# A late piece's stores as operations of their own, and a new order for the second half of a fast block product

## The chip, the cores and the metric

The kernel runs on one core of a Trainium2 chip. The core has a tensor engine (PE), a vector engine (DVE), a scalar engine (ACT, ScalarE), GpSimd (POOL), a queue that mostly issues transfers (SP, SyncE), and 16 DMA engines. Each engine runs its own list of instructions in order; semaphores make one wait for another. The metric is the time of one execution in device microseconds, lower being better.

## The reference

Two stages, one fed by the other. The first is attention with a polynomial sketch: for 4 batches, 4 heads, 1088 positions and 32 dimensions, queries and keys become 64 products of 8 + 8 projections, and

```python
a = np.einsum('rd,bhsd->bhsr', S1, x)
b = np.einsum('rd,bhsd->bhsr', S2, x)
phi = np.einsum('bhsi,bhsj->bhsij', a, b).reshape(*x.shape[:-1], r * r)
...
num = np.einsum('bhsf,bhfd->bhsd', q_p, kv)
den = np.einsum('bhsf,bhf->bhs', q_p, z)[..., None] + 1e-06
```

The quotient, laid out as (batch, 1088, 128), is the x of the second stage, which mixes positions with two matrices of 1088 by 1088:

```python
theta = x @ w_theta
zr, zi = x * np.cos(theta), x * np.sin(theta)
y = np.einsum('ts,bsd->btd', w_tok_r, zr) + np.einsum('ts,bsd->btd', w_tok_i, zi)
u = x + y
out = u + np.maximum(u @ w_ch, 0.0)
```

## The kernel before

The positions are cut into 8 full chunks of 128 and a tail of 64. The two mixing matrices are read as 17 rows of weights (8 of the real, 8 of the imaginary part, one row with both tails), kept in the chip's memory as `rows[i]`. Batches 0 and 1 are mixed directly: 17 products of each span of 384 positions add up in an accumulator bank (`mix_row`), a copy of the sum gets x added by a transfer that accumulates (`join`), and `finish` multiplies by `w_ch`, applies the relu and stores.

Batches 2 and 3 (`PAIR`) are mixed together by `winograd`, which replaces eight block products by seven. It splits the output positions into two halves of 544 (`HT`) and the sources into real and imaginary parts. `zsub` makes differences of the z blocks, `asum` sums and differences of the weight blocks (both on DVE), `product` runs each of the seven block products as two parts of widths 384 and 160 (`PARTS`), eight steps each, in an accumulator bank, and `add` adds a finished bank to x on DVE. Products 1 and 2, then 5, 6, 3, 7 and 4 follow from each other through the banks and the blocks that they reuse. `done(b, h)` calls `finish` for half h of batch b, in pieces of 384 and 160 positions. `finish` runs a product with `w_ch` on PE, a relu with add on DVE (L319), a turn on DVE (`turn`, L1240) and stores of 32 columns each (`store`, L1236). Batch 3's half 0 is special: its piece of 160 goes through `finish_turned` (turns on PE at L1274, a copy on ACT at L1281, relu, two plain stores at L1286), and for its piece of 384, with which the kernel ends, `ends` is true, and the stores are issued inside the same operation as the turn, one on ScalarE, one on SyncE, two on GpSimd.

In the turned batches (1 to 3) x is brought into place through memory: a DVE transpose, a store to `far` on SyncE (L1098) and a fetch of four transfers on SyncE (`fetch`, L1102). DVE multiplies it by the cosine and the sine; that is the z of `winograd`.

Nothing is scheduled when the kernel is built. Every step is recorded as an operation with its engine and what it reads and writes; `ORDER` is a written-out list that says in which order the operations are issued, and so gives each engine its own list, and `SLOTS` says which buffer of its class each temporary takes. A product is a call of `mm` (L332), a DVE step with two operands one of `tt` (L312) or `stt` (L319), so that most rows of the profile carry these helpers' lines and are told apart by their tiles.

Of the kernel before, what the change touches and what calls it, by code (L numbers as in the profile page):

```python
# [77 lines left out]
)  # L78
GAPS = {11: 3, 57: 3, 79: 3, 110: 1, 203: 8, 153: 1, 77: 5, 86: 2, 163: 1}
SLOTS = (  # L80
# [11 lines left out]
)  # L92
WARM = 0
LOAD_LEAD = 60.0
# [37 lines left out]
class Layout:  # L132
# [17 lines left out]
    def buf(self, cls, shape, dt, name):  # L150
        b = Buf(cls, shape, dt, name)
        self.bufs.append(b)
        return b
# [92 lines left out]
def kernel(  # L246
# [56 lines left out]
    V, A, G, T, SY = nc.vector, nc.scalar, nc.gpsimd, nc.tensor, nc.sync  # L303
# [14 lines left out]
    def stt(o, a, s, b, op0, op1, eng=None):  # L318
        (eng or V).scalar_tensor_tensor(out=o, in0=a, scalar=s, in1=b, op0=op0, op1=op1)  # L319
# [8 lines left out]
    def vop(n, fn, w, r, due=None, two=False, lk=0):  # L328
        op("V", dve2(n) if two else dve(n), fn, w, r, due, lk=1 if two else lk)

    def mm(o, lhs, rhs, start, stop):
        T.matmul(o, lhs, rhs, start=start, stop=stop, skip_group_check=True)  # L332
# [871 lines left out]
    def mix_out(b, span, yp, due):  # L1204
        g, t0, t1 = span
        xt = xT[b]
        at("out", b, "_", g)
        w = t1 - t0
        xkeys = cells(xt, t0, t1)
        uT = buf("g1", (GW,), F32, "uT")  # L1210
        u = lambda: uT()[:, :w]
        if UDMA[b]:
            op("A", act(w), lambda: A.copy(u(), yp()[:, :w]), [uT], [yp])  # L1213
            join(u, lambda: xt()[:, t0:t1], [uT], xkeys, ADD_FLY2)
        else:
            vop(w, lambda: tt(V, u(), xt()[:, t0:t1], yp()[:, :w], ALU.add), [uT], xkeys + [yp])
        finish(b, t0, w, u, [uT], due)

    def finish(b, t0, w, u, keys, due, ot=None):
        whole = ot is not None  # L1220
        ends = whole and t0 < HT and b == PAIR[1]
        last = not whole or ends or (t0 + w) % HT == 0
        if ends and t0:
            finish_turned(b, t0, w, u, keys, due)
            return
        po = buf("ps", (GW,), F32, "po")
        at0 = t0 % HT if whole else 0
        if not whole:
            ot = buf("g1", (GW,), F32, "ot")
        op("P", w * 4 / 2400 + 0.01, lambda: mm(po()[:, :w], w2()[:, 1], u(), True, True), [po], keys + [w2], hold=[ot])  # L1230
        vop(w, lambda: stt(u(), po()[:, :w], 0.0, u(), ALU.max, ALU.add), keys, [po])
        s0, n = (t0 + w - HT, HT) if whole and not ends else (t0, w)

        def store(E, f0, f1):
            for f in range(f0, f1):
                E.dma_start(out[b, s0:s0 + n, f * SQ:(f + 1) * SQ].rearrange("(c j) i -> j c i", j=SQ),  # L1236
                            ot()[f * SQ:(f + 1) * SQ, :n].rearrange("j (c i) -> j c i", i=SQ))

        def turn():
            V.transpose(out=ot()[:, at0:at0 + w], in_=u())  # L1240
            if ends:
                store(A, 0, 1)
                store(SY, 1, 2)
                store(G, 2, 4)

        vop(w, turn, [(ot, at0)], keys)
        if not last or ends:
            return

        if b == PAIR[0] and t0 >= HT and w == GW:  # L1250
            op("S", w * P * 2 / 100e3, lambda: store(SY, 0, 2), [], [ot], due, lk=2)
            op("A", 0.46, lambda: store(A, 2, 3), [], [ot], due, fly=2.1)
            op("G", 0.9, lambda: store(G, 3, 4), [], [ot], due, fly=2.0)
        elif b == PAIR[0] and t0 >= HT:
            op("A", 0.92, lambda: store(A, 0, 1), [], [ot], due, fly=2.1)
            op("S", w * P * 2 / 100e3, lambda: store(SY, 1, 3), [], [ot], due, lk=1)
            op("G", 0.9, lambda: store(G, 3, 4), [], [ot], due, fly=2.0)
        elif b in PAIR:
            op("S", w * P * 2 / 100e3, lambda: store(SY, 0, 2), [], [ot], due, lk=2)
            op("A", 0.92, lambda: store(A, 2, 4), [], [ot], due, fly=2.1)  # L1260
        elif b and t0 < 2 * GW:
            op("S", w * P * 4 / 100e3, lambda: (store(SY, 0, 2), store(G, 2, 4)), [], [ot], due, lk=4)
        else:
            op("S", w * P * 4 / 100e3, lambda: store(SY, 0, DM // SQ), [], [ot], due, lk=4)

    def finish_turned(b, t0, w, u, keys, due):
        po, pu = (buf("ps", (GW,), F32, x) for x in ("po", "pu"))
        n = w // 2
        yb = buf("g1", (2 * DM,), F32, "yb")
        y = lambda: yb()[:n]  # L1270

        def turned():
            for c in range(2):
                T.transpose(pu()[:n, c * DM:(c + 1) * DM], u()[:, c * n:(c + 1) * n], ident())  # L1274

        def products():
            for c in range(2):
                mm(po()[:n, c * DM:(c + 1) * DM], u()[:, c * n:(c + 1) * n], w2()[:, 1], True, True)

        op("P", 0.2, turned, [pu], keys, hold=[yb])  # L1280
        op("A", act(2 * DM), lambda: A.copy(y(), pu()[:n, 0:2 * DM]), [yb], [pu])  # L1281
        op("P", 0.35, products, [po], keys + [w2])
        vop(2 * DM, lambda: stt(y(), po()[:n, 0:2 * DM], 0.0, y(), ALU.max, ALU.add), [yb], [po])

        def store(E, c):
            E.dma_start(out[b, t0 + c * n:t0 + (c + 1) * n, :], y()[:, c * DM:(c + 1) * DM])  # L1286

        op("S", w * P * 2 / 100e3, lambda: store(SY, 0), [], [yb], due, lk=2)
        op("A", 0.92, lambda: store(A, 1), [], [yb], due, fly=2.1)
# [193 lines left out]
```

## Time and profile before

| | |
|---|---|
| median of three runs | 218.51 us (218.4 to 219.59) |
| profiled execution, its own time | 217.77 us |
| its span, first to last instruction | 216.0 us |
| PE busy | 207.4 us, 96% |
| DVE busy | 180.7 us, 84% |
| ACT busy | 113.5 us, 53% |
| POOL busy | 38.5 us, 18% |

The page gives for each engine its busy time, then the span in slices, the DMA queues, the chain of work that ended last, and the costliest groups of instructions with what ended the idle time before them. Times inside the span are counted from its start. The profiled execution took 1.77 us more than its span. A row of the timeline has the start, the length, the engine, the line, the operation, what it writes and reads, and in brackets the idle time of the engine before it and what ended that.

### The profile page before, as it was taken

The numbers are of one execution on the slowest core, as the hardware profiler recorded it, in microseconds if no ns is written. First come the engines' busy times: TensorE is split into PE (matmuls) and PEld (weight loads), VectorE is DVE, ScalarE is ACT, GpSimd is POOL, SyncE is SP. The second block draws the span as 40 slices with busy tenths as digits, with TensorE's granted clock in tenths as the row PEclk, the third lists the DMA queues.
The fourth block names the chain that finished last, engine by engine and source line by source line (L and its number), as shares of the span: only waits on it lengthen the run. The fifth ranks groups of instructions, "written<-read, shape, count | busy, mean of one in ns | idle before, by whom it ended". The sixth has DMA issues, their size and how long they took to land.

```text
span 216.0 us, 5299 instructions
## 1 busy us (share of the span) xinstructions
PE 207.4 (96%) x2140; PEld 150.2 (70%) x2140; DVE 180.7 (84%) x359; ACT 113.5 (53%) x240; POOL 38.5 (18%) x89
## 2 busy tenths in 40 slices
PE   7999999999999999999999999999999999999990
PEld 7777798968767666775656676576766776677660
DVE  1799999999999998998999999979497799955151
ACT  4899999999999896796711423159500000000000
POOL 1182640307300000930003010000220020020013
PEclk9999999999999999999999999999999999999998
DMA  6999999996996994192002244022660012110433
GB/s 226 395 417 418 380 362 420 429 324 143 347 244 230 421 429 177 56 323 49 0 0 36 40 141 113 0 39 108 137 109 0 0 39 50 17 36 4 76 62 67
DMA packets 28044, 37.06 MB, mean 172 GB/s; under 512 B 20564, under 2 KB 23044, under 8 KB 25844
## 3 DMA queue, kind: packets, MB, share of 16 engines
q1 hardware_dynamic: 22868, 31.86, 42.2%
q0 software_dynamic: 1552, 3.25, 7.1%
q10 hardware_dynamic: 3600, 1.62, 2.8%
q8 instruction: 17, 0.28, 0.5%
q14 instruction: 7, 0.06, 0.1%
HBM read 29.84 MB, written 4.00 MB: 157 GB/s over the span
## 4 chain that ended last, share of the span: by engine, by line
PE 58%; DMA 17%; DVE 10%; ACT 9%; issue 3%; SPq 1%; POOL 0%; POOLq 0%; DVEq 0%; ACTq 0%
PE ps L332 54%; DMA zs<-w_tok 11%; DMA zs<-far 2%; DMA st<-s 2%; DVE big L312 2%; ACT big L578 2%; PE ps L951 2%; ACT big L626 2%; DMA far<-zs 1%; DVE g L312 1%; PE ps L1053 1%; DVE big L316 1%; ACT g L726 1%; ACT big L576 1%; PE ps L361 1%
## 5 line engine op out<-in xcount | busy, mean ns | idle before, releaser
L332 PE MATMUL ps<-big,zs 128*128 128x384 f32 (+2 forms) x380 | 108.8, 435 | 0.0
L332 PEld LDWEIGHTS ps<-big,zs 128*128 128x128 f32 x380 | 67.1, 191 | 34.2 <-issue 0.9
L1281 ACT COPY g<-ps 80x256 f32<-80x256 f32 x1 | 0.4, 367 | 54.1 <-PE ps L1274 54.1
L332 PE MATMUL ps<-big,big 128*32 128x32 f32 (+2 forms) x352 | 21.8, 235 | 0.0
L312 DVE CUSTOM_DVE_ANT_0 big<-big,big 128x2176 uint16<-128x2176 uint16 x17 | 21.6, 1281 | 0.1
L578 ACT ACTIVATE big<-zs 128x1088 int32<-128x1088 uint32 (+1 forms) x18 | 21.3, 1190 | 0.7 <-DMA zs<-w_tok 0.7
L576 ACT ACTIVATE big<-zs 128x1088 f32<-128x1088 f32 x17 | 20.9, 1229 | 0.7 <-DMA zs<-w_tok 0.7
L332 PEld LDWEIGHTS ps<-big,big 128*32 128x32 f32 (+1 forms) x352 | 14.9, 125 | 5.6 <-issue 1.0
L312 DVE TENSOR_TENSOR big<-big,big 128x544 f32<-128x544 f32 x24 | 16.7, 713 | 0.1
L326 POOL DMA_DIRECT2D g<-big x6 | 5.3, 1070 | 56.0 <-ACT g L1213 56.0
L1236 POOL DMA_DIRECT2D out<-g x8 | 5.0, 631 | 50.3 <-DVE g L1240 36.0
L312 DVE TENSOR_TENSOR zs<-zs,g 128x384 f32<-128x384 f32 (+2 forms) x24 | 9.9, 449 | 4.0 <-DMA zs<-far 4.0
L316 DVE TENSOR_SCALAR big<-big 128x1088 int32<-128x1088 int32 x17 | 12.3, 721 | 0.0
L361 PE MATMUL ps<-idle 128*128 128x112 bf16 (+1 forms) x67 | 10.0, 312 | 1.3 <-POOL idle L363 1.3
L312 DVE TENSOR_TENSOR g<-lv 128x768 f32<-128x768 f32 x12 | 11.1, 950 | 0.1
L312 DVE TENSOR_TENSOR big<-big,hf 128x1152 f32<-128x1152 f32 x8 | 10.7, 1351 | 0.0
L332 PE MATMUL ps<-mf,big 128*128 128x96 f32 (+1 forms) x72 | 10.0, 278 | 0.4 <-DVE big L312 0.4
L332 PE MATMUL ps<-sbk,g 128*128 128x64 f32 x72 | 10.1, 276 | 0.3 <-ACT g L726 0.3
L332 PE MATMUL ps<-w,big 128*128 128x128 f32 (+1 forms) x76 | 10.2, 278 | 0.0
L332 PEld LDWEIGHTS ps<-w,big 128*128 128x128 f32 (+1 forms) x76 | 9.4, 190 | 0.5
L1139 ACT ACTIVATE g<-g 128x384 f32<-128x384 f32 x12 | 6.3, 532 | 6.7 <-DVE g L319 6.7
L332 PEld LDWEIGHTS ps<-sbk,g 128*128 128x128 f32 x72 | 9.0, 191 | 0.8 <-ACT g L726 0.6
(198 smaller groups left out, 353.0 us busy)
## 6 DMA issues: line engine op xcount, KB each, us to landing
zs<-w_tok SPq DMA_DIRECT2D x17, 1088.0 KB, 10.6
big<-k_l SPq DMA_DIRECT2D x5, 576.0 KB, 12.6
big<-v_l SPq DMA_DIRECT2D x4, 576.0 KB, 15.4
big<-q_l SPq DMA_DIRECT2D x3, 576.0 KB, 10.4
big<-hf POOLq DMA_DIRECT2D x3, 576.0 KB, 9.7
far<-zs SPq DMA_DIRECT2D x3, 576.0 KB, 3.8
zs<-far SPq DMA_DIRECT2D x12, 144.0 KB, 4.1
big<-k_l ACTq DMA_DIRECT2D x2, 576.0 KB, 4.2
```

Source lines behind the costliest of these rows:

```text
L312: eng.tensor_tensor(out=o, in0=a, in1=b, op=f)
L316: (eng or V).tensor_scalar(out=o, in0=a, scalar1=s1, scalar2=s2, op0=op0, **kw)
L326: op("G", 0.9, lambda: G.dma_start(dst(), src(), accum_op=ALU.add), w, r, fly=fly)
L332: T.matmul(o, lhs, rhs, start=start, stop=stop, skip_group_check=True)
L361: T.matmul(nowhere()[:, :n], idle()[:, 0:P], idle()[:, :n], start=True, stop=True, skip_group_check=True)
L576: op("A", 0.22 + n * 0.0009, lambda: A.activation(dfn(), words_of(raw(), n)[1].bitcast(F32), AF.Prelu, scale=2.0**-112, alpha=-(2.0**32)), ...
L578: op("A", 0.22 + n * 0.0009, lambda: A.activation(stp(), words_of(raw(), n)[0].bitcast(U32), AF.Copy, scale=2.0**-29), [stp], [raw])
L626: op("A", act(n) + 0.1, lambda: A.activation(flat(r()), kc(), AF.Square, accum_out=km()[:, 1:2]), [r, (km, 1)], [kx])
L726: op("A", act(GW), lambda kT=kT, tr=tr: A.copy(kT().rearrange("p c n -> p (c n)"), tr()), [kT], [tr])
L951: T.transpose(tr()[:, i * P:(i + 1) * P], x()[:, g * GC + i].rearrange("p h d -> p (h d)"), ident())
L1139: op("A", act(GW), lambda cs=cs: A.activation(cs()[:, 0], cs()[:, 1], AF.Abs), [(cs, 0)], [(cs, 1)])
L1236: E.dma_start(out[b, s0:s0 + n, f * SQ:(f + 1) * SQ].rearrange("(c j) i -> j c i", j=SQ), ot()[f * SQ:(f + 1) * SQ, :n].rearrange("j (c i) ...
```

## The change

Two things change. `finish` no longer treats the stores of the wide piece of batch 3's half 0 apart: they become operations of their own, as for the other pieces of the pair, two stores on SyncE and two on ScalarE, and GpSimd issues none of them. And the last 260 entries of `ORDER` and some 30 of `SLOTS` are new. The numbers of `ORDER` name operations in the order in which they are recorded; there are 1003 instead of 1001, and those behind the two added operations are counted on.

```diff
         def turn():
             V.transpose(out=ot()[:, at0:at0 + w], in_=u())
-            if ends:
-                store(A, 0, 1)
-                store(SY, 1, 2)
-                store(G, 2, 4)

         vop(w, turn, [(ot, at0)], keys)
-        if not last or ends:
+        if not last:
             return
```

From `ORDER` (its last rows):

```diff
-    912, 979, 980, 958, 959, 823, 826, 827, 969, 913, 970, 971, 972, 973, 974, 975, 976, 977, 981, 982, 983, 824, 623,
-    829, 960, 965, 828, 984, 978, 914, 989, 900, 990, 901, 902, 985, 986, 903, 991, 993, 987, 904, 915, 919, 920, 992,
-    964, 988, 995, 921, 905, 996, 922, 997, 994, 1000, 916, 923, 998, 917, 924, 999, 918,
+    963, 964, 829, 911, 965, 966, 981, 978, 979, 982, 983, 980, 984, 912, 991, 992, 913, 914, 985, 915, 993, 967, 994,
+    986, 987, 988, 989, 921, 923, 990, 997, 995, 922, 924, 925, 926, 996, 998, 999, 1000, 1002, 1001,
```

Each engine's list keeps its instructions and gets another sequence from the turn of batch 3's x onwards:

- PE starts product 1 earlier, puts the output products of batch 1 earlier, runs product 1 and half of product 2 ahead of product 5, and most of product 3's wide part ahead of product 7. At the end the order was: product 3's wide part, the turns for batch 3's narrow piece, batch 2's narrow output product, the narrow piece's products, the wide piece's product. It is now: product 4's narrow part, the turns and the products of batch 3's narrow piece, batch 2's narrow output product. The wide piece's product stands among the last steps of product 7.
- DVE's `zsub`, `asum` and `add` steps follow PE's new order; the outputs of batch 1 come before batch 3's product with cosine and sine.
- ACT does the sines of chunks in another sequence and copies batch 1's sums out earlier.
- SyncE issues the four stores of batch 0's last piece ahead of the fetch of batch 3's turned x instead of behind it. GpSimd issues batch 1's joins in another sequence and earlier, and two stores fewer.

33 rows, old and new, of tables (ORDER, SLOTS) are left out of this document.

## The prediction

> **What bounds the kernel now.** I read the page first, then the busy times of the last stretches, then what the tensor engine (PE) waits for, then the last steps one by one. The page says which engine can matter:
>
> ```profile
> span 216.0 us, 5299 instructions
> ## 1 busy us (share of the span) xinstructions
> PE 207.4 (96%) x2140; PEld 150.2 (70%) x2140; DVE 180.7 (84%) x359; ACT 113.5 (53%) x240; POOL 38.5 (18%) x89
> ```
>
> The two orders are the same, instruction for instruction, up to the fetch of batch 3's turned x, at about 152 us of the span; PE's lists part at 147 us. What has been given another buffer ahead of that (the squares of q of batch 3, rows 10 and 13 of the weights and two step buffers) takes buffers whose last users are done by then. So only the last third of the span can change, and there the busy times by stretch are (columns: stretch, length, then PE, weight loads, DVE, ACT, POOL busy with their counts, the granted clock, DMA share, GB/s):
>
> ```profile
> 170.00:180.00 10.00, 10.00 (x51) 7.73 (x50) 9.64 (x19) 0.00 (x0) 1.34 (x2) 1.00 0.10 21
> 180.00:190.00 10.00, 10.00 (x43) 6.83 (x42) 9.87 (x20) 0.00 (x0) 0.00 (x0) 1.00 0.21 36
> 190.00:200.00 10.00, 10.00 (x48) 7.35 (x47) 5.01 (x12) 0.00 (x0) 1.23 (x2) 1.00 0.13 25
> 200.00:210.00 10.00, 10.00 (x47) 7.00 (x45) 3.36 (x8) 0.37 (x1) 0.61 (x1) 1.00 0.43 72
> 210.00:216.00 6.00, 0.35 (x2) 0.00 (x0) 1.52 (x4) 0.00 (x0) 1.84 (x3) 0.89 0.30 60
> ```
>
> PE is busy for 10.00 of every 10 us at full clock: in this order no product waits for anything. The chain that ended last says the same, one unbroken piece of PE and then stores and the closing steps:
>
> ```profile
> 140.00 68.72 PE ps L332 x330
> ...
> 212.49 0.60 POOLq L1479
> ```
>
> A new order of the same products therefore can't make this stretch shorter. It can (a) open holes in PE, which cost their length, or (b) change the 7 us behind the last bulk product. The prediction is (b) less (a).
>
> **The end, before.** PE, DVE and the rest in their own timelines (start, length, engine, line, tile):
>
> ```profile
> 203.87 0.81 PE L332 MATMUL ps<-big,w 128*128 128x384 f32 x2
> 204.52 4.20 PE L332 MATMUL ps<-big,zs 128*128 128x384 f32 x16
> 208.56 0.38 PE L1274 MATMUL ps<-ident,big 128*80 128x128 f32 x2
> 208.78 0.44 PE L332 MATMUL ps<-big,w 128*128 128x160 f32 x2
> 209.05 0.60 PE L332 MATMUL ps<-w,big 128*80 128x128 f32 x4
> 209.49 0.86 PE L332 MATMUL ps<-big,w 128*128 128x384 f32 x2
> ```
> ```profile
> 208.12 0.32 DVE L312 TENSOR_TENSOR big<-big,ps 128x160 f32<-128x160 f32 x1 [1.96 <-PE ps L332]
> 208.76 0.62 DVE L319 SCALAR_TENSOR_TENSOR big<-ps,even,big 128x384 f32<-128x384 f32 x1 [0.32 <-PE ps L332]
> 209.30 0.31 DVE L319 SCALAR_TENSOR_TENSOR big<-ps,big 128x160 f32<-128x160 f32 x1
> 209.76 0.42 DVE L319 SCALAR_TENSOR_TENSOR g<-ps,g 80x256 f32<-80x256 f32 x1 [0.15 <-PE ps L332]
> 210.11 0.33 DVE L1240 STREAM_TRANSPOSE g<-big 128x160 f32<-128x160 f32 x1
> 210.38 0.56 DVE L319 SCALAR_TENSOR_TENSOR big<-ps,big 128x384 f32<-128x384 f32 x1
> 210.97 0.58 DVE L1240 STREAM_TRANSPOSE g<-big 128x384 f32<-128x384 f32 x1
> ```
> ```profile
> 208.98 0.37 ACT L1281 COPY g<-ps 80x256 f32<-80x256 f32 x1 [54.09 <-PE ps L1274]
> 210.65 1.33 SPq L1236 DMA_DIRECT2D out<-g  x3
> 210.73 0.59 POOL L1236 DMA_DIRECT2D out<-g  x1 [3.93 <-DVE g L1240]
> 211.85 1.24 POOL L1236 DMA_DIRECT2D out<-g  x2 [0.52 <-DVE g L1240]
> ```
> ```profile
> L1479 POOLq DRAIN  x3: 34/93/2937, 212.3 to 215.7; - x3
> ```
>
> Starts in a row give what PE takes: 0.65 us for a product of width 384 (203.87 to 204.52), 0.27 for 160 (208.78 to 209.05), 0.22 for the pair of turns (208.56 to 208.78), 0.44 for their two products (209.05 to 209.49). A result is there about 0.17 after its stream (0.44 long, next start after 0.27), and DVE takes it up 0.04 later. The last bulk product streams until 208.56. The wide piece (batch 3, rows 0 to 383) then goes last of all: its product from 209.49, DVE 0.56 and 0.58 until 211.55, POOL's two stores until 211.85 + 1.24 = 213.09, POOL's drain until 212.3 + 2.94 = 215.2, and 0.8 to the end.
>
> **Part 1: the wide piece leaves the end.** In the new order its product stands at about 196.3, among the last of product 7, its turn at about 198.4, and its four stores are two on SyncE and two on ScalarE. PE's work is the same, so the last bulk product now ends 0.65 later: 208.56 + 0.65 = 209.21. It is 160 wide and belongs to batch 2. Behind it, step by step: result 209.21 + 0.17 + 0.04 = 209.42, add 0.32, done 209.74. PE meanwhile does the turns and products of batch 3's narrow piece, 0.22 + 0.44, until 209.87, then batch 2's last product, result at 209.87 + 0.44 = 210.31. DVE has the narrow piece from 210.07 and frees itself 0.35 later (209.76 to 210.11), at 210.42; relu 0.31, done 210.73; turn from 210.76, 0.33, done 211.09, against 211.55: **0.46 earlier**. POOL starts 0.29 behind a turn (210.44 to 210.73), at 211.38, and has one store of 0.59 instead of two of 1.24: done 211.97 against 213.09, **1.12 earlier**. The landing, from the DMA table of the last 8 us (KB each, us from issue to landing):
>
> ```profile
> out<-g POOLq DMA_DIRECT2D x2, 48.0 KB, 2.1
> ...
> out<-g POOLq DMA_DIRECT2D x1, 20.0 KB, 1.9
> ```
>
> The last store lands at 211.38 + 1.9 = 213.3, against 211.85 + 0.62 + 2.1 = 214.6: 1.3 earlier. SyncE's last two stores (0.44 each, from 211.1) start by 211.6 and land, with the largest of these prices, by 213.7, and ScalarE's one earlier; with the drain still to come they don't end last. The drain isn't seen alone: if it follows the landing or the issue it ends 1.1 to 1.3 earlier; if its 2.94 us are fixed from its start, it ends 211.38 + 0.44 + 2.94 = 214.76, only 0.46 earlier. I take the first, since a wait that is longer than every other closing step looks like one for a landing: **-1.15 us**, with -0.46 as the small end.
>
> By the Trainium skill, "DMA: Bandwidth & Descriptors", section "Anatomy of one DMA — SWDGE (gpsimd) path", a GpSimd transfer takes 2.0 us and its bytes at 436 GB/s, an estimate of 2.05 us for 20 KB and 2.11 for 48; the trace has 1.9 and 2.1, so by the page the gain would be 0.1 less.
>
> **Part 2: the four stores.** Two on SyncE at about 199.3 and two on ScalarE at about 199.0, 0.4 to 0.5 us each. Both queues next wait for later results; ScalarE's only engine work left is the copy at L1281, 10 us later (it sat idle for 54 us ahead of it). Behind them wait other stores alone. Cost 0. Were that cover gone, ScalarE's two would hold up the copy by at most 1 us.
>
> **Part 3: the new order, holes in PE.** I laid the new lists out engine by engine with the durations of the rows. DVE's rows overlap by 0.08 (208.76 + 0.62 against 209.30), so an add of width 544, its commonest step here, takes 0.71 - 0.08 = 0.63:
>
> ```profile
> L312 DVE TENSOR_TENSOR big<-big,big 128x544 f32<-128x544 f32 x24 | 16.7, 713 | 0.1
> ```
>
>  No product comes out late; the least room is at the accumulator that is read and used again. Between product 7's last of width 384 and product 4's first stand 0.27 + 0.65 + 0.27 = 1.19 us of PE, and the add in between needs 0.17 + 0.62 + 0.08 = 0.87: 0.3 to spare. Ahead of batch 2's wide product, four of width 160 (1.09) against the same 0.87: 0.2. At the very end 0.66 against 0.17 + 0.32 + 0.08 = 0.57: 0.1. Everything else has 0.8 us or more. So 0, and each us that an operand comes late beyond that costs one. The three places where queues were moved past each other:
>
> ```profile
> 148.96 0.34 SPq L1098 DMA_DIRECT2D far<-zs  x1
> 152.26 1.74 SPq L1102 DMA_DIRECT2D zs<-far  x4
> 154.04 1.96 SPq L1236 DMA_DIRECT2D out<-g  x4
> ```
> ```profile
> 155.50 0.58 DVE L312 TENSOR_TENSOR zs<-zs,g 64x128 f32<-64x128 f32 x2 [2.47 <-DMA zs<-far]
> 156.69 1.70 DVE L312 TENSOR_TENSOR zs<-zs,g 128x256 f32<-128x256 f32 x4 [0.62 <-DMA zs<-far]
> ```
> ```profile
> g<-big POOLq DMA_DIRECT2D x1, 160.0 KB, 4.2
> ```
>
> SyncE: the four stores of batch 0's last piece (1.96 us) now stand ahead of the fetch of the turned x. They fit: SyncE waits from 149.3 to 152.26 for the far copy anyway. Today the fetch has landed at 156.69, and DVE sat waiting for it (2.47 and 0.62 us). In the new order DVE has other work first (the adds and the outputs of batch 1) and comes to it at about 158.3; product 5 starts at 161.3, when its first operand is 1.4 us old. So the fetch may come 1.6 us late for nothing and about 3 us late before PE stands. POOL: batch 1's joins go earlier, the last needed one at about 150.0; with the longest landing shown, 4.2, it is there at 154.2, and its product starts at 155.5. The adds that wait behind the fetch on DVE wait less than today.
>
> Against this speaks the Trainium skill, "DMA: Bandwidth & Descriptors", section "Queues, rings and completion order": an engine takes the descriptors of one queue in ring order, so the fetch must come out behind the stores that SyncE issued first. By that rule the fetch is late by what is left of the stores at 152.26, at most their 1.96 us; no run here shows it yet, and the sum stays as it is.
>
> **Sum.** -1.15 us on the profiled execution: span 216.0 to 214.85, its own time 217.77 to 216.6. The median of the three runs, 218.51, lies 0.74 above the profiled one; the same step from it gives 217.4. The runs may hold short waits on the fetch that the profiled one lacks, and the new order has 3 us of room there, so I put 217.3.
>
> **Rivals.**
> *The drain is fixed* (2.94 us from its start). For it: one long record, begun before POOL's last store. Against: nothing else in the closing steps is longer than 0.1 us. It gives -0.46: 218.1. Chance 0.19.
> *The waits of the timed runs go too.* The lowest run is 218.4, 0.63 above the profiled one; if that is the fetch coming late, the new order hides it, -1.15 - 0.63: 216.7. Against: a constant difference explains it as well. Chance 0.18.
> *Slower: DVE becomes the bound.* From 158.3 to 191.1 DVE has hardly a gap in the new order (in the old one 9.64 and 9.87 of 10 us from 170 to 190), and the first narrow part of product 7 starts only 1.0 us behind the add that frees its accumulator. If DVE comes 1.0 us late there, by the fetch's 1.96 us of stores and the joins that now share the DMA engines with it, each further us opens a hole in PE. To end slower it must be more than 1.0 + 1.15 = 2.2 us late, and 3.2 late for a loss of 0.5%: 219.6. For it: DVE is the second busiest engine and its work is moved in bulk. Against: the durations of its rows vary little, and PE's room before is no larger at its tightest places. Chance 0.13.
> *It does nothing*: another store, SyncE's or ScalarE's, ends as late as POOL's did: 218.4. Against: they have 0.3 us in hand above. Chance 0.05.
>
> **How the numbers follow.** The forecast has 0.45. About 0.5% (1.1 us) is what a measurement of this kernel can tell from no change, and the forecast lies on that edge: I give it 0.33 beyond and 0.12 within, since of the two doubts (the timed runs' waits, the page's 0.1) the first is larger. Faster: 0.33 + 0.18 + 0.03 of the drain's 0.19 = 0.54. Within: 0.12 + 0.16 + 0.05 = 0.33. Slower: 0.13. The range goes from 216.3 (both gains, and 0.4 for the spread of runs) to 218.7 (no gain at all, and 0.2); it leaves out most of the slower case and the tails.
>
> **What would show it.** In the changed profile: PE 10.00 in every stretch from 150 to 209; the last narrow turn of L1240 ending near 211.1; one POOL store behind it and the drain ending near 214.0 (near 214.8 by the first rival); DVE no longer waiting for the fetch. Wrong it is if a group of PE or its weight loads shows idle time with DVE or a DMA as releaser behind 150 us.

## The result, and the profile after

| | before | after |
|---|---|---|
| median of 15 runs each, same chip | 218.17 us (217.34 to 219.59) | 216.98 us (216.21 to 217.97) |
| ratio, 95% interval | 1 | 0.9944 (0.9924 to 0.9965) |
| a second comparison, 8 runs of after against 27 | 218.07 us | 216.88 us, 0.9929 (0.9906 to 0.9953) |
| profiled execution, its own time | 217.77 us | 217.18 us |
| its span | 216.0 us | 215.4 us |

The change gains 1.2 us of 218 in both comparisons. The profiled executions alone differ by 0.6 only, and the reason stands ahead of the change: the far copy of batch 3's x (L1098 on SyncE), up to which the two kernels issue the same, went out at 148.96 us before and at 149.62 after. From that instruction to the end of the span it is 67.03 before and 65.78 after, **1.25 us less**. All profiles below are compared in this way, from the far copy on.

The page of after, top:

```profile
span 215.4 us, 5299 instructions
## 1 busy us (share of the span) xinstructions
PE 206.7 (96%) x2140; PEld 149.3 (69%) x2140; DVE 181.0 (84%) x359; ACT 113.6 (53%) x240; POOL 37.2 (17%) x87
```

The last stretches of after (columns as in the prediction):

```profile
170.00:180.00 10.00, 10.00 (x41) 6.69 (x40) 8.67 (x16) 0.00 (x0) 0.00 (x0) 1.00 0.01 2
180.00:190.00 10.00, 10.00 (x40) 6.55 (x39) 8.80 (x19) 0.00 (x0) 1.23 (x2) 1.00 0.10 20
190.00:200.00 10.00, 10.00 (x46) 7.08 (x45) 5.05 (x11) 0.00 (x0) 0.00 (x0) 1.00 0.00 0
200.00:210.00 10.00, 10.00 (x52) 7.60 (x51) 3.69 (x9) 0.00 (x0) 0.13 (x1) 1.00 0.48 77
210.00:215.40 5.40, 0.98 (x9) 0.74 (x6) 1.32 (x4) 0.37 (x1) 1.08 (x2) 1.00 0.35 67
```

PE is still busy for 10.00 of every 10 us: the new order opened no hole. What changed lies in the last row. The timeline of after, first the transfers of batch 3's x with the DVE work that depends on them, then two waits of DVE, then the end:

```profile
149.62 0.34 SPq L1098 DMA_DIRECT2D far<-zs  x1
150.01 2.49 SPq L1236 DMA_DIRECT2D out<-g  x4
152.79 1.89 SPq L1102 DMA_DIRECT2D zs<-far  x4
...
159.00 0.98 DVE L312 TENSOR_TENSOR zs<-zs,g 128x384 f32<-128x384 f32 x2
...
172.01 0.73 DVE L312 TENSOR_TENSOR big<-big 128x544 f32<-128x544 f32 x1 [1.27 <-PE ps L332]
...
189.83 0.32 DVE L319 SCALAR_TENSOR_TENSOR big<-ps,big 128x160 f32<-128x160 f32 x1 [1.17 <-PE ps L332]
...
209.86 0.38 PE L1270 MATMUL ps<-ident,big 128*80 128x128 f32 x2
...
210.06 0.32 DVE L312 TENSOR_TENSOR big<-big,ps 128x160 f32<-128x160 f32 x1 [0.49 <-PE ps L332]
210.08 0.60 PE L332 MATMUL ps<-w,big 128*80 128x128 f32 x4
210.28 0.37 ACT L1277 COPY g<-ps 80x256 f32<-80x256 f32 x1 [52.84 <-PE ps L1270]
...
210.52 0.46 PE L332 MATMUL ps<-big,w 128*128 128x160 f32 x2
...
211.46 0.34 DVE L1240 STREAM_TRANSPOSE g<-big 128x160 f32<-128x160 f32 x1
211.84 0.82 SPq L1236 DMA_DIRECT2D out<-g  x2
...
212.10 0.59 POOL L1236 DMA_DIRECT2D out<-g  x1 [1.61 <-DVE g L1240]
```

The last turn is a narrow one (160), ended at 211.80, and one store of GpSimd follows it. Its landing, from the DMA table of the last 8 us, and GpSimd's drains (count; shortest, mean and longest in ns):

```profile
out<-g POOLq DMA_DIRECT2D x1, 20.0 KB, 1.8
```
```profile
L1475 POOLq DRAIN  x3: 34/102/2528, 212.1 to 215.1; - x3
```

The store lands at 212.10 + 1.8 = 213.9; the drain ends at 212.08 + 2.53 = 214.61, 0.7 behind it. Before, the drain was 2.94 long and ended at 215.2. It is not fixed. In after it is also hardly the last step any more: by the records of the trace SyncE's closing checks are over at 214.65, 0.04 behind the drain, where before they were over at 214.78, 0.44 ahead of it.

### The profile page after: what moved, and what is told of

Its sections match the earlier page's. It is cut to its first block, busy times and chain, and to the rows that moved or that the text cites. A ratio compares the mean times of both kernels' runs of the same rounds, so it can differ in the third digit from the quotient of the medians.

```text
span 215.4 us, 5299 instructions
## 1 busy us (share of the span) xinstructions
PE 206.7 (96%) x2140; PEld 149.3 (69%) x2140; DVE 181.0 (84%) x359; ACT 113.6 (53%) x240; POOL 37.2 (17%) x87
## 4 chain that ended last, share of the span: by engine, by line
PE 40%; DVE 15%; ACT 15%; issue 14%; DMA 11%; SPq 1%; POOL 1%; POOLq 0%; DVEq 0%; ACTq 0%
PE ps L332 36%; DVE big L312 6%; DMA zs<-w_tok 5%; ACT big L578 4%; DMA zs<-far 3%; ACT big L576 2%; DMA st<-s 2%; PE ps L951 2%; ACT big L626 2%; DMA far<-zs 1%; DVE g L312 1%; DVE zs L312 1%; DVE big L316 1%; PE ps L1053 1%; ACT g L726 1%
## 5 line engine op out<-in xcount | busy, mean ns | idle before, releaser
L1236 POOL DMA_DIRECT2D out<-g x6 | 3.8, 634 | 52.3 <-DVE g L1240 52.3
```

## The experiments

One theory is that of the prediction: the gain is the wide piece leaving the end, and the rest costs nothing, because PE has its operands in time. The rivals: the gain comes from DVE's waits for the fetch; the move of the fetch behind four stores costs something that the gain hides; the end is fixed by closing steps. A fourth question is what the new order buys besides the end.

The table has, for each profiled run, the us from the far copy to the end of the last turn, to the end of the last DMA packet and the issuer of that store, and to the end of the span (read from the records of the trace); then the idle time that the profile lists for PE behind 146 us, and the timed ratio to before. e1 to e4 share one chip and one set of runs of before (median 217.7), e5 to e8 another (218.43), e9 to e12 a third (218.07). Each kernel's line numbers are its own, shifted by a few.

| run | far copy at | last turn | last packet | end | PE idle | ratio (95%) |
|---|---|---|---|---|---|---|
| before | 148.96 | 62.59 | 65.15 GpSimd | 67.03 | 0 | 1 |
| after | 149.62 | 62.18 | 63.89 GpSimd | 65.78 | 0 | 0.9944 (0.9924 to 0.9965) |
| e1_stores_only | 149.35 | 62.59 | 64.82 SyncE | 66.57 | 0 | 0.9973 (0.9949 to 0.9997) |
| e2_order_only | 148.84 | 62.19 | 63.90 GpSimd | 65.81 | 0 | 0.9947 (0.9919 to 0.9974) |
| e3_end_only | 148.09 | 62.40 | 64.12 GpSimd | 66.04 | 0 | 0.9925 (0.9895 to 0.9955) |
| e4_fetch_first | 148.17 | 62.19 | 63.93 GpSimd | 65.78 | 0 | 0.9935 (0.9902 to 0.9968) |
| e5_before_late_fetch | 150.62 | 64.45 | 66.99 GpSimd | 68.89 | 1.62 | 1.0073 (1.0041 to 1.0104) |
| e6_after_late_fetch | 149.94 | 62.42 | 64.14 GpSimd | 65.99 | 0 | 0.9956 (0.9921 to 0.9991) |
| e7_before_more_dve | 150.13 | 64.58 | 67.09 GpSimd | 68.97 | 1.25 | 1.0092 (1.0056 to 1.0128) |
| e8_after_more_dve | 150.37 | 62.19 | 63.89 GpSimd | 65.77 | 0 | 0.9939 (0.9913 to 0.9966) |
| e9_last_first | 149.40 | 62.10 | 64.22 SyncE | 65.96 | 0.20 | 0.9965 (0.9943 to 0.9987) |
| e10_no_pool_at_end | 149.21 | 62.19 | 63.90 ScalarE | 65.65 | 0 | 0.9940 (0.9916 to 0.9964) |
| e11_last_first_no_pool | 150.02 | 62.10 | 64.37 ScalarE | 66.10 | 0.20 | 0.9962 (0.9942 to 0.9982) |
| e12_after_again | 148.74 | 62.19 | 63.89 GpSimd | 65.76 | 0 | 0.9929 (0.9906 to 0.9953) |

### The three parts of the change

**Only the stores** (the code of the change with before's order and buffers; the two new operations, 919 and 920, stand last, and the numbers behind them are counted on; the last row of `ORDER`):

```diff
-    964, 988, 995, 921, 905, 996, 922, 997, 994, 1000, 916, 923, 998, 917, 924, 999, 918,
+    966, 990, 997, 923, 905, 998, 924, 999, 996, 1002, 916, 925, 1000, 917, 926, 1001, 918, 919, 920,
```

> The old order and buffers; the wide piece's four stores are own operations at the end of the list, two on SyncE and two on ScalarE, and GpSimd has none of them. Theory E (all of the gain is the wide piece leaving the end of the kernel): the turn still ends at about 211.5, the second store of SyncE starts near 212.1 and lands near 214.0 instead of 214.5, so -0.3 to -0.8 us: 217.4 to 217.9, ratio about 0.998. Theory F (the gain is room for the fetch of batch 3's x in the middle): 0, ratio 1.000. Theory S (the gain is that GpSimd issues two stores fewer): all of it, -1.2 us, ratio 0.9945.

The end came 0.46 earlier. The wide piece still goes last, and now its second store on SyncE is the late one. Timeline of this run:

```profile
211.04 1.90 SPq L1241 DMA_DIRECT2D out<-g  x4
211.12 0.59 POOL L1241 DMA_DIRECT2D out<-g  x1 [3.94 <-DVE g L1245]
...
211.36 0.58 DVE L1245 STREAM_TRANSPOSE g<-big 128x384 f32<-128x384 f32 x1
```
```profile
L1480 POOLq DRAIN  x3: 34/102/2597, 211.1 to 215.7; - x3
```

GpSimd's drain was over at 211.09 + 2.60 = 213.69, yet the span ended at 215.92, 1.75 behind the last packet of SyncE's store (214.17). So it is the last landing, whoever issued it, that sets the end.

**Only the order** (after's order and buffers; against after, the stores of the wide piece are back inside its turn, two of them on GpSimd):

```diff
             V.transpose(out=ot()[:, at0:at0 + w], in_=u())
+            if ends:
+                store(A, 0, 1)
+                store(SY, 1, 2)
+                store(G, 2, 4)

         vop(w, turn, [(ot, at0)], keys)
-        if not last:
+        if not last or ends:
```

> The new order and buffers, but the wide piece's stores are issued inside the turn as before (one ScalarE, one SyncE, two GpSimd). Theory E: the stores lie 12 us ahead of the end, so the same as the changed kernel: -1.2 us, 217.0, ratio 0.9945; from the issue of the far copy of batch 3 (near 149) to the end of the span 65.8 us against 67.0. Theory S: 0, ratio 1.000. Theory F: as the changed kernel too.

65.81 against after's 65.78: with the wide piece out of the end, who issues its stores makes no difference. So the 0.46 of the run before comes from moving stores that stand at the end, and in the new order the new operations are worth nothing by themselves.

**Only the end** (before's kernel, its stores included; only the last 53 entries of `ORDER`, behind 913 (the expectation counts 59), are put into after's manner: the wide piece's product among product 4's wide steps, product 4's narrow steps last; and that product takes another accumulator):

```diff
-    912, 979, 980, 958, 959, 823, 826, 827, 969, 913, 970, 971, 972, 973, 974, 975, 976, 977, 981, 982, 983, 824, 623,
-    829, 960, 965, 828, 984, 978, 914, 989, 900, 990, 901, 902, 985, 986, 903, 991, 993, 987, 904, 915, 919, 920, 992,
-    964, 988, 995, 921, 905, 996, 922, 997, 994, 1000, 916, 923, 998, 917, 924, 999, 918,
+    910, 911, 912, 979, 980, 958, 959, 823, 826, 827, 969, 913, 900, 901, 902, 903, 904, 970, 971, 824, 623, 829, 960, 965,
+    828, 964, 905, 972, 916, 917, 918, 973, 974, 975, 976, 977, 981, 982, 978, 914, 983, 989, 915, 990, 984, 985, 986, 987,
+    991, 993, 992, 994, 919, 920, 988, 921, 995, 922, 996, 923, 924, 997, 998, 1000, 999,
```

> The old order until about 196 us of the span, the old stores; only the last 59 operations are put otherwise: product 3's wide part and the wide piece's output go ahead of product 4, product 4's narrow part comes last. The fetch and everything behind it until then stand as before. Theory E: -1.15 us, 217.0, ratio 0.9945; last narrow turn ending near 211.1 if the far copy is issued at 148.96; no idle time on PE behind 150 us. Theory F: less than half of it, ratio 0.998 or more.

0.99 of the 1.25 is there with 53 of the 260 new entries. The timeline says where 0.2 is missing:

```profile
209.06 0.37 ACT L1286 COPY g<-ps 80x256 f32<-80x256 f32 x1 [55.04 <-DVE big L317]
...
210.15 0.34 DVE L1245 STREAM_TRANSPOSE g<-big 128x160 f32<-128x160 f32 x1
...
210.79 0.60 POOL L1241 DMA_DIRECT2D out<-g  x1 [1.26 <-DVE g L1245]
```

ACT's copy starts 60.97 behind the far copy, where after has 60.66; it was released by DVE's last add here, by PE's turns there. The relu behind it, and the last turn, are 0.2 later. Why the copy waits for DVE here isn't settled. The timed ratio (0.9925) is as good as that of after; 0.2 us is less than the runs can tell.

### The queue: is the fetch late behind the stores?

In after the four stores of batch 0's last piece stand ahead of the fetch on SyncE. Here the fetch goes first again:

```diff
-    777, 639, 640, 763, 764, 664, 534, 778, 758, 759, 813, 760, 769, 784, 765, 535, 761, 779, 615, 837, 840, 793, 520,
+    777, 639, 640, 763, 764, 664, 534, 778, 758, 759, 813, 760, 769, 784, 765, 761, 535, 779, 615, 837, 840, 793, 520,
```

> The changed kernel, but SyncE issues the fetch of batch 3's turned x ahead of batch 0's four stores again. Theory E: no change against the changed kernel, 217.0, ratio 0.9945, since DVE comes to the x later than it lands in both. Theory F: part of the gain goes or comes, 0.3 us or more. If stores hold back a fetch behind them in the same queue, the fetch here lands up to 2 us sooner after the far copy's issue than in the changed kernel, and DVE still has no wait for it.

```profile
148.17 0.34 SPq L1097 DMA_DIRECT2D far<-zs  x1
151.04 1.75 SPq L1101 DMA_DIRECT2D zs<-far  x4
152.84 5.13 SPq L1235 DMA_DIRECT2D out<-g  x9
```

The end is the same, 65.78. In the trace the first packet of the fetch ran 0.96 us behind its issue here and 1.18 in after: the stores, issued from 150.01 to 152.50, delay it by 0.2. By the Trainium skill, "DMA: Bandwidth & Descriptors", section "Queues, rings and completion order", a DMA engine takes the descriptors of one queue in ring order; the traces agree in direction, and the price here is 0.2 us, a tenth of the 1.96 that the prediction allowed for. That the fetch is also issued 0.3 us later in after (3.17 us behind the far copy, 2.87 here) can't be put down to the stores: before, with no store between the two, it was 3.29.

### The room: what the order tolerates

**A later fetch**, in the old order and in the new: a copy of the same size into spare memory is issued ahead of it.

```diff
+            spare = None
+            if b == PAIR[1]:
+                spare = hop.tile([P, NC * P], F32, tag="spare", name="spare")
+
             def fetch():
+                if spare is not None:
+                    SY.dma_start(spare, far())
```

> The kernel before, with one more transfer: ahead of the four fetches of batch 3's turned x SyncE copies the 576 KB of it from memory to memory, to a place that nothing reads. The fetch then comes later by this copy, 1.5 to 2.5 us. Theory R (the old order has little room for the fetch, about 0.9 us from the profiled landing to the first product 5 that waits): PE stands for 0.6 to 1.6 us ahead of product 5, near 160, with DVE's difference as releaser; from the far copy's issue to the end 67.6 to 68.6 us instead of 67.0, ratio 1.003 to 1.007. Theory N (the room is the same in both orders): the same loss as the changed kernel with this copy.

> The changed kernel with the same extra copy ahead of the fetch. Theory R: about 3 us of room, so no idle time on PE behind 150 us; from the far copy's issue to the end 65.8 us as without the copy; ratio 0.9945. Theory N: it loses what the kernel before loses, 0.6 us or more.

The fetch's last packet came 2.75 us later in the old order (9.61 behind the far copy against 6.86) and 2.79 later in the new one (9.88 against 7.09). The timelines, old order first:

```profile
154.17 0.53 SPq L1106 DMA_DIRECT2D spare<-far  x1
154.80 1.96 SPq L1108 DMA_DIRECT2D zs<-far  x4
...
159.86 0.58 DVE L312 TENSOR_TENSOR zs<-zs,g 64x128 f32<-64x128 f32 x2 [5.18 <-DMA zs<-far]
```
```profile
153.09 0.55 SPq L1106 DMA_DIRECT2D spare<-far  x1
153.74 1.95 SPq L1108 DMA_DIRECT2D zs<-far  x4
...
160.83 1.03 DVE L312 TENSOR_TENSOR zs<-zs,g 128x384 f32<-128x384 f32 x2 [1.44 <-DMA zs<-far]
```

DVE waits 5.18 us (and 1.04 once more) in the old order, 1.44 in the new. PE's waits behind 146 us, old order (none is listed for the new one):

```profile
PE ps L332 <- DVE big L312: 1.6, 1, 1.6
```

The end moves by 1.86 in the old order, a little more than the 0.6 to 1.6 expected, and by 0.21 in the new one, where nothing was expected: no hole is listed there, but from 12.7 us behind the far copy on each product of PE starts 0.24 later than in after.

**More work for DVE**: the step that forms operand "2" in `zsub` is done three times over.

```diff
-vop((c1 - c0) * P, lambda c0=c0, c1=c1: tt(V, dst[0](c0, c1), x[0](c0, c1), y[0](c0, c1), ALU.subtract),
+vop((c1 - c0) * P, lambda c0=c0, c1=c1: [tt(V, dst[0](c0, c1), x[0](c0, c1), y[0](c0, c1), ALU.subtract)
+                                         for _ in range(3 if name == "2" else 1)],
```

> The kernel before, with DVE's three differences of the second set (two of width 384, one of 256) each done three times over, the same values written again: 2.6 us more DVE work between 158 and 176. Theory R: the old order has DVE full from 170 to 190 and little room, so PE stands for 0.7 to 1.5 us in all near products 6 and 3; from the far copy's issue to the end 67.7 to 68.5, ratio 1.003 to 1.007. Theory N: no loss, or the same as in the changed kernel.

> The changed kernel with the same 2.6 us of DVE work added. Theory R: DVE waits for PE between 160 and 190 for longer than that, and each result has 0.3 us or more left: no idle time on PE, 65.8 us from the far copy's issue to the end, ratio 0.9945. Rival of the prediction (DVE becomes the bound where product 7's narrow part starts, 1.0 us of room): 1.5 us of idle PE there, 67.3.

The three places in the new order:

```profile
163.54 1.74 DVE L312 TENSOR_TENSOR big<-zs,big 128x384 f32<-128x384 f32 x3
...
165.83 1.73 DVE L312 TENSOR_TENSOR big<-zs,big 128x384 f32<-128x384 f32 x3
...
170.86 1.34 DVE L312 TENSOR_TENSOR big<-zs,big 128x256 f32<-128x256 f32 x3
```

With single steps of 0.56, 0.55 and 0.42 they are 3.28 us more work. The new order ends at 65.77, unchanged; the old one 1.94 later, where 0.7 to 1.5 were expected. Its waits of PE:

```profile
PE ps L332 <- DVE big L319: 0.6, 1, 0.6
PE ps L332 <- DVE big L312: 0.6, 1, 0.6
```

These holes are 1.25 of the 1.94. The rest shows when the starts of the products in this run and in before are set side by side, both counted from the far copy. PE falls behind by 0.89, 0.20 and 0.90 us, at 28.4, 30.5 and 33.9 us: 1.99 in all, as much as the last turn is late (64.58 against 62.59). The listed holes are shorter, since a product stands in the profile with 0.49 us, while the next one starts 0.32 behind it; a small delay, like the middle one, leaves no hole at all. So the new order takes up 3.28 us of added work on DVE without a loss, where the old one loses 1.9; but nothing in the ordinary run asks for it. In the new order DVE comes up to 2.79 us later than in after, and its own waits for PE (in after 0.42, 1.27 and 1.17 us between 163 and 190 us) take this up; each product of PE starts within 0.01 us of where it did.

### What sets the end now

Three variants of the last steps, and after once more beside them. First, batch 2's narrow output product, relu, turn and stores ahead of the products of batch 3's narrow piece:

```diff
-    989, 921, 923, 990, 997, 995, 922, 924, 925, 926, 996, 998, 999, 1000, 1002, 1001,
+    989, 995, 996, 921, 922, 990, 997, 923, 998, 999, 1000, 1001, 1002, 924, 925, 926,
```

> The changed kernel with the last steps in another sequence: batch 2's narrow output product, its relu, turn and stores go ahead of the products, relu and stores of batch 3's narrow piece; the same operations, nothing left out. Theory (the end is the chain behind the last narrow turn): the turn ends some 0.2 us earlier, since the narrow piece's two products (0.44 us) no longer stand ahead of it, and the stretch from the far copy to the end of the span goes from 65.78 to about 65.6, unless the stores of batch 3's narrow piece, now issued behind, land last. Rival (the end is fixed by SyncE's own closing checks): 65.8, unchanged. Time about 216.8 by the theory, 217.0 by the rival.

```profile
210.22 0.54 PE L331 MATMUL ps<-big,w 128*128 128x160 f32 x2 [0.20 <-DVE big L311]
...
212.43 0.38 SPq L1281 DMA_DIRECT2D out<-g  x1
```

The turn came 0.08 earlier, not 0.2 as expected: the output product, put first, now waits 0.20 for DVE's add. And the stores of batch 3's narrow piece, put last, land last: 65.96 instead of 65.76.

Second, no store of GpSimd at the end:

```diff
-            op("A", 0.92, lambda: store(A, 0, 1), [], [ot], due, fly=2.1)
-            op("S", w * P * 2 / 100e3, lambda: store(SY, 1, 3), [], [ot], due, lk=1)
-            op("G", 0.9, lambda: store(G, 3, 4), [], [ot], due, fly=2.0)
+            op("A", 0.92, lambda: store(A, 0, 2), [], [ot], due, fly=2.1)
+            op("S", w * P * 2 / 100e3, lambda: store(SY, 2, 4), [], [ot], due, lk=1)
+            op("G", 0.9, lambda: None, [], [ot], due, fly=2.0)
```

> The changed kernel with the last narrow piece's four stores as two on ScalarE and two on SyncE, none on GpSimd; nothing left out. Theory (the drain on GpSimd follows the landing of GpSimd's own last store, and with it the end): the drain becomes short and is over by about 211, and SyncE's second store, issued about 212.3 (by the changed kernel's clock) and landing 1.5 to 2 us later, sets the end: 65.78 from the far copy becomes 65.4 to 65.9. Rival (the drain is long whatever GpSimd did last, 2.5 us from where it starts): the drain keeps 2.5 us but starts earlier. Time 216.6 to 217.1; the comparison says whether GpSimd's store or SyncE's is the slower way out.

```profile
L1475 POOLq DRAIN  x3: 34/93/2907, 209.4 to 214.6; - x3
```
```profile
211.42 0.82 SPq L1236 DMA_DIRECT2D out<-g  x2
211.43 0.86 ACTq L1236 DMA_DIRECT2D out<-g  x2
```

The drain now starts at 209.44, with GpSimd's earlier store of 48 KB, and is over at 212.34, 2.5 us before the end. It did not become short, as I had expected; it ends 0.63 us behind the landing of that earlier store. ScalarE's second store ends its packets 63.90 behind the far copy, where GpSimd's did at 63.89: an even exchange but for 0.1 us of closing steps.

Third, both edits, and after again:

> Both edits together: the narrow piece of batch 2 ahead of batch 3's at the end, and its stores on ScalarE and SyncE alone; nothing left out. Theory: the two gains are in a row (turn 0.2 earlier, then a landing 0 to 0.4 earlier), 65.78 from the far copy becomes 65.2 to 65.7, time about 216.6. Rival (something else closes the span, unchanged by both): 65.8 and 217.0.

> The changed kernel once more, as the comparison for the three before it and as a second measure of the whole change on the same chip: by the first one 0.9944 of before, stretch from the far copy to the end 65.78. If the profile again ends 65.7 to 65.9 behind the far copy, wherever that copy falls, the gain is in that stretch and the rest is scatter.

Both edits together end at 66.10, where 65.2 to 65.7 was expected: the gains don't add up. The likely reason, not tested by itself, is that the second edit puts two stores each on the queues that the first one fills. After again ends at 65.76, with its far copy 0.88 earlier than in the first profile: 215.4 and 214.5 us of span for one and the same kernel. None of the three variants is shown to be better than after.

## Why the prediction was right

The forecast was -1.15 us, 217.3 us; the median is 216.98, and -1.19 against the runs of before beside it. The 0.3 between the two is the base: the first three runs of before had a median of 218.51, all fifteen 218.17.

Step by step, on the clock of after (0.66 added to the prediction's times, by the two far copies):

- *PE stays full.* 10.00 in every full stretch, and PE passes to the last turns at 209.86; foretold 209.21 + 0.66 = 209.87. Shown.
- *The last turn ends 0.46 earlier.* Foretold 211.75, measured 211.80; by the far copy it is 0.41 earlier. The 0.05 is the relu at L319 ahead of it, at 210.78 instead of 210.73.
- *One store of GpSimd behind the last turn instead of two.* Foretold start 212.04 and landing 213.96; measured 212.10 and 213.9. Of the 1.25 the turn has 0.41, and the way from the turn to the last packet 0.85 (2.56 before, 1.71 after).
- *The drain follows the landing.* Foretold end 214.66, measured 214.61. The rival of a fixed 2.94 us falls: 2.53 here, 2.60 in e1_stores_only, 2.91 in e10_no_pool_at_end with a store of 48 KB. The choice was right, but one reading given for it was not: among the closing steps of before the drains of PE's weight loads (0.96) and of DVE (0.62) are longer than 0.1 us too. And the forecast had the drain alone at the end; in after SyncE's closing checks end beside it, so a drain that is shorter still would by itself gain hardly more.
- *The page's 0.1.* By the Trainium skill, "DMA: Bandwidth & Descriptors", section "Anatomy of one DMA — SWDGE (gpsimd) path", 20 KB were estimated at 2.05 us; the trace of after has 1.8, where the forecast took 1.9 from before. The measurement decides against the page's smaller gain.
- *The order itself costs nothing, and the stores nothing.* Shown by e2_order_only (65.81 against 65.78) and e4_fetch_first (65.78). DVE, which waited 3.1 us for the fetch before, doesn't wait for it in after.
- *The timed runs' waits go too* (217.3 rather than 217.4, and the rival of 216.7). Not so: the timed gain, 1.2, is the gain of the end and no more, and e3_end_only, in which DVE still waits 3.2 us for the fetch, times as well as after. Those waits cost PE nothing. The fetch that does come late from one execution to another is an earlier one, of batch 1, ahead of the change in both orders (last section).
- *DVE becomes the bound.* It didn't. One premise of that rival was wrong: that DVE has hardly a gap from 158.3 to 191.1. It waits 1.27 and 1.17 us for PE there and is busy 8.67 and 8.80 of 10 us, less than the 9.64 and 9.87 of before. The 1.0 us of room at product 7's narrow part was never tried: e8_after_more_dve has DVE 2.79 us late at 170 us of after's clock, but the add that frees that bank, at 191.34 in after, came only 0.13 later, since DVE's waits had taken up the rest. These waits are what kept the rival away. For the fetch it was put at 3 us before PE stands, and e6_after_late_fetch, 3.0 later than before's, lost 0.2.

The mechanism is shown by taking the change apart: its end alone brings 0.99, its order alone 1.22, its stores alone 0.46, and all together 1.25. The parts overlap, so they don't add up.

## What to carry to other kernels

Where the bound engine is full up to its last step, look at what is done behind that step, and end on the smallest piece: here the last turn and the store behind it went from a width of 384 to 160, and that brought the gain, while the rest of the new order added 0.26 us in the profiles, nothing that the timed runs show, and room that the ordinary run doesn't use. Compare two profiles from the last instruction that both share, not from the start of the span: the common part differed by up to 2.5 us from one execution to another. When a last store is taken off one queue, work out which store lands last then; each of three further variants only handed the end to another one.

## What the runs showed of the hardware that I had not expected

**The way out has a fixed length.** From the last DMA packet to the end of the span it took 1.73 to 1.75 us where SyncE or ScalarE had issued that store (4 runs), and 1.85 to 1.92 where GpSimd had (10 runs). Before and after both belong to the second kind. The trace of after shows the steps: GpSimd's store landed at 213.94, SyncE's ten closing checks ran from 213.96 on, one each 0.06 us, and with its drains SyncE was done at 214.65; the span ended 0.75 later.

**The stretch ahead of the change scatters.** The far copy went out between 148.09 and 150.62 us in 14 profiles, though the instructions up to it are the same; within the four profiles of one chip, e9 to e12, between 148.74 and 150.02. Waits of PE ahead of 146 us, in the first profile of after and in the second:

```profile
PE ps L415 <- DVE m L434: 0.9, 1, 0.9
PE ps L332 <- DVE zs L312: 0.8, 1, 0.8
```
```profile
PE ps L415 <- DVE m L434: 0.6, 1, 0.6
```

The wait for DVE's `zs` is 0.8 us in one and missing in the other, and the far copies differ by 0.88. This scatter is as large as the effect that was to be measured. The traces show the step at which it arises: DVE's first product of batch 1's x with the cosine, which waits for the fetch of that x (first and second profile of after):

```profile
100.67 0.56 DVE L312 TENSOR_TENSOR zs<-zs,g 128x384 f32<-128x384 f32 x1 [1.71 <-DMA zs<-far]
```
```profile
99.78 0.56 DVE L312 TENSOR_TENSOR zs<-zs,g 128x384 f32<-128x384 f32 x1 [1.00 <-DMA zs<-far]
```

In the 14 profiles this product starts between 99.13 and 101.66 us, and the far copy of batch 3 follows it by 48.95 or 48.96 us in every one. Why the fetch of batch 1 lands at different times was not tried.
